# Forming three modulation vectors later, and layer-norm statistics on a second engine, in a hand-ordered long-convolution and MLP block

## The chip, the cores and the metric

The kernel runs on one core of a Trainium2 chip. A core has a matrix engine (PE, whose weight loads are listed apart as PEld), a vector engine (DVE), an activation engine (ACT), a general engine (POOL, also called GpSimd) and an engine that mostly issues transfers (SP); 16 DMA engines move data. PE writes to PSUM, and DVE or ACT carry its results from there to SBUF ("eviction"). The metric is the device time of one execution in microseconds (us). Before the change it is 314.69 us, the median of three runs (313.75 to 314.99).

## The reference, cut to what matters

```python
def reference(A_q, A_k, A_v, A_shift_k, A_ssm_k, A_ssm_D, B_x, B_w1, B_w2, B_w3, B_w4, c, w_mod):
    # _A_ref: k is convolved with 4 taps, kv = k_shift * v, then a long
    # causal convolution of kv with ssm_k (through an FFT of length 4096),
    # plus kv * ssm_D; result times q
    # _B_ref: layer norm, @w1, gelu, a token shift by quarters of the channels, @w2,
    # residual; layer norm, @w3, gelu, @w4, residual
    x = A_q                                             # 1 x 2048 x 640, bf16
    mod = (_silu(c) @ w_mod).reshape(c.shape[0], 6, 1, -1)
    sa, ca, ga, sb, cb, gb = (mod[:, i] for i in range(6))     # shortened
    h = _layernorm(x, axis=-1) * (1 + ca) + sa
    x = x + ga * _A_ref(h, A_k, A_v, A_shift_k, A_ssm_k, A_ssm_D)
    h = _layernorm(x, axis=-1) * (1 + cb) + sb
    x = x + gb * _B_ref(h, B_w1, B_w2, B_w3, B_w4)
    return x
```

Three of the six vectors (ga, ca, sa) are needed for the query side of the convolution block; the other three (cb, sb, gb) first when the MLP block begins.

## The kernel before

The kernel is a list of tasks. Each task names the engine or engines that may run it, what it reads and writes, and a function that records its instructions. A string `ORDER` holds one word for each task: its number, the letter of its engine (P for PE, A for ACT, D for DVE, G for POOL, S for SP), and for PE tasks the PSUM places that it takes (four places of two banks each). The instructions are recorded in just that order; each engine works through its own list in order and waits for what it needs.

```python
    def evac(dst, src, n, ps, w, eng=("ACT", "DVE")):       # eviction, on either engine
        ...
        return add(eng, {"ACT": ca(n), "DVE": cd(n)}, f, (), w, use=ps)
```

The transform of the convolution is made of matrix products. Stage 1 and stage 2 turn the filter (`s`) and then kv into spectra; the filter's spectrum lies in R3 (10 blocks of 2048 columns), that of kv in R5. In between, PE makes the shift of k (`k_shift`), whose result DVE multiplies by v and transposes in 32x32 blocks.

```python
    def stage2(XSd, dreg):
        for k in range(32):
            ...   # 4 matmuls of 64 x 64 x 320 each, then one 128x640 eviction
    def mod_half(i, j, hf):        # half of modulation vector j
        w, wk = wm[i % 3]          # three buffers, in RH and RK
        dma("SP", 410, lambda q: q.dma_start(w, mod_d[:, :, j * D + 320 * hf:j * D + 320 * hf + 320]), w=[wk], rate=250.0)
        ...                        # 5 matmuls of 320 columns, one write of modv (copy, +1 or product)
    def mods():
        for i, j in enumerate((2, 1, 0, 4, 3, 5)):
            for hf in range(2):
                mod_half(2 * i + hf, j, hf)
    def ln1_stats(A):              # 16 tiles of 128 x 640
        ...
            for i in range(2):
                nc.vector.bn_stats(st[:, i, :], x_all[:, A, i * 320:(i + 1) * 320])
            nc.vector.bn_aggr(mv1[:, A, :], st[:])
        add("DVE", 1.1, f, ...)
    x_load(0, 8)
    x_load(8, NT)
    for a0, a1 in ((0, 4), (4, 6), (6, 8), (8, 10), (10, 12), (12, 14), (14, 16)):
        for A in range(a0, a1):
            ln1_stats(A)
        ln1_fin(a0, a1)            # on POOL: 1/sqrt(var + eps) and -mean/sqrt(var + eps)
    mods()
```

Then come the spectral products and the first inverse step, for two halves h of five blocks b each:

```python
    def inverse1(h, b):
        i = h * ND + b
        kx, xs = R3[:, 2048 * i:2048 * i + 2048], R5[:, 2048 * i:2048 * i + 2048]
        ky, kk = KSY[i % 4]        # four buffers; ky is kx with its partition halves swapped, by DMA
        ...
        for T, k_, deps, wr in ((TA, kx, [kxk], ka), (TB, ky, [kk], kb)):
            add("DVE", 1.24, ...)  # one 128x2048 product each
        for w8 in range(2):
            ...                    # 16 matmuls of 128 columns, one 128x1024 eviction
```

The second inverse step (`inverse2`) returns to tokens. `make_q` forms the normalized and modulated query tile (a normalization, one multiply, one add); `chain_a` gates the convolution with it and adds the residual (L689, L692), `chain_b` normalizes and modulates with cb and sb (L703, L704), `chain_c` normalizes again and transposes. Then the MLP: `mm_w1`, `mm_w2` (eviction L832), `mm_w3` (gelu on ACT, L861) and `mm_w4` (evictions L899 to L905, with gb), for eight groups of two tiles.

```python
    for g in range(8):
        ra = chain_a(g)
        rb = chain_b(g, ra)
        chain_c(g, rb)
        ...
        mm_w1(g)
        if g >= 1:
            mm_w2(g - 1)
        if g >= 2:
            mm_w3(g - 2)
            mm_w4(g - 2)
```

Of the kernel before, what the change touches and what calls it, by code (L numbers as in the profile page):

```python
# [18 lines left out]
ND = D // P  # L19
# [7 lines left out]
19G 0S 18D 20D 21G 23D 22D 24A 56G 27G 29D 28D 25A 2S 31A 30A 36G 37G 68G 69D 26G 90P:0 91A 86P:1 6S 87A 88P:2 89A 4S 72G 73D 104P:3 105A 102P:0  # L27
106P:1 107A 38G 39G 40A 3S 70D 71D 96P:2 97A 98P:3 103D 99A 5S 74G 75D 49G 1S 66G 94P:0 50G 8S 118P:1 9S 114P:2 115A 10S 92P:3 93A 95D 41G 52D 51D 32D
53A 116P:0 110P:2 119D 84P:3 42G 11S 43G 34S 7S 54A 33G 44A 85A 111A 67D 117D 122P:1 123D 112P:3 113A 108P:2 109A 100P:0 101D 76P:3 77A 203S 45G 47S
46S 78P:1 79D 35S 82P:2 83A 80P:0 81A 120P:3 170P:1 283D 121D 178P:2 55G 171A 176P:0 179A 180P:1 177A 65G 181D 194P:3 198P:2 195A 199D 234S 48S 202S  # L30
148P:0 57G 58G 200S 149A 142P:1 201S 143D 182P:3 183A 140P:2 141D 231S 12S 13S 144P:0 145A 188P:1 14S 136P:3 15S 189A 137D 162P:2 163A 156P:0 157D
164P:1 165A 150P:3 151D 190P:2 191A 168P:0 174P:1 175A 169D 196P:3 197A 138P:2 139D 160P:0 161A 16S 186P:1 158P:3 159A 146P:2 184P:0 185A 187D 17S
166P:1 167A 147D 192P:3 193A 235P:2 236A 152P:0 213D 232P:1 153A 233A 208D 154P:3 155A 172P:2 288P:0 173A 294P:1 295A 289A 284D 126P:3 298P:2 302P:1
209D 124P:0 214D 59G 60A 299A 303A 210D 296P:2 297A 130P:1 300P:2 301A 127D 125D 290P:3 291A 128P:0 61G 211D 62G 63G 64A 237S 285D 304P:2 306P:3 307A
131D 134P:1 129D 286D 305A 310P:0 311A 215G 132P:3 312P:2 313A 135D 133D 238P:0 239D 292P:1 293A 314P:3 315A 316P:2 287D 243S 244P:0 245D 240S 318P:1
317D 319A 326P:3 327D 320P:0 321A 324P:1 325A 322P:2 308P:0 241P:3 212G 393G 246S 247P:1 309A 323D 352P:2 353A 348P:0 242D 248D 486D 380P:3 381A 349D
252S 253P:1 254D 330P:2 331A 346P:0 347D 338P:3 339A 356P:1 357A 334P:2 335D 392S 390P:0 391A 354P:3 355D 376P:1 362P:2 489D 205S 350P:0 351D 377A
249S 250P:3 251D 363A 261S 487D 366P:1 367A 255S 382P:2 383D 332P:0 333A 340P:3 341A 262P:1 263A 217D 258S 344P:0 342P:2 343A 328P:3 329A 256P:1 345D
257D 374P:2 375A 480D 358P:0 276S 359D 364P:3 365A 388P:1 389A 259P:2 260A 275G 281S 481D 279G 277G 264S 368P:0 278G 282G 280G 272S 386P:3 273G 270S
268S 271G 274G 490D 384P:1 387A 385A 360P:2 369D 378P:0 379A 269S 361D 372P:3 373A 336P:1 370P:2 371A 267S 265P:0 492A 216D 337D 401G 266A 400S 394D  # L40
395D 408S 409G 396P:3 398P:2 399A 493D 491D 402D 494D 397A 403D 410D 404P:1 405A 411D 406P:0 418D 412P:2 413A 417G 414P:3 415A 416S 419D 426D 422P:1
423A 424S 420P:2 421A 425G 427D 434D 433G 407A 432S 435D 430P:3 431A 428P:1 442D 441G 438P:2 436P:0 437A 440S 443D 446P:3 444P:0 450D 448S 449G 451D
447A 456S 439A 429A 454P:3 457G 458D 483A 459D 464S 452P:2 466D 460P:1 445A 462P:0 453A 465G 467D 206S 455A 463D 470P:2 471D 461A 207S 468P:3 469A
488D 495P:01 496A 497A 498P:23 500A 482D 479G 474S 484D 485D 204S 220D 226D 219D 519D 520D 508P:01 218G 499A 543D 522D 523D 524A 544D 477S 525G 521A
510A 526G 557D 554D 472S 555D 558D 560D 475S 501G 602D 559A 502P:32 509A 556A 545D 546D 503A 531D 527D 532D 528D 504A 529D 530A 561G 533D 535D 511P:10
534A 505P:32 603D 605D 606D 547D 512A 536G 566A 540D 541P:1 513A 537D 538P:0 562A 563D 542A 539D 478G 221G 564D 551P:1 567D 607A 604A 608G 506A 609G
568D 565A 569A 570D 552A 610D 611D 517S 612D 571G 572D 575D 549P:0 550A 553G 476S 573P:3 574D 613A 514S 576P:1 577D 586P:0 614D 615D 616D 618D 617A
619G 587A 584P:3 585A 578D 579D 507A 580D 548D 672D 623D 624P:1 625A 620D 621P:0 622A 473S 591P:3 634P:2 588P:1 675D 676D 677A 673D 678D 592D 674A
679G 593A 635A 589D 590A 684D 632P:0 518G 633A 636P:3 685D 594G 686D 687A 581D 680D 681D 682D 683A 595G 599D 600P:1 596D 637D 601D 638A 597P:2 639P:0
598A 656P:3 657A 650P:1 688D 582D 640D 641A 689G 225D 583D 516S 223D 690A 652P:2 691S 740D 642G 643G 644D 692D 693S 647D 648P:0 649D 653A 654P:3 626D  # L50
627D 651A 645P:0 628D 743D 744D 745A 702P:2 700P:1 703A 701A 646D 724P:0 720P:2 741D 742A 227G 746G 704P:1 655A 222D 224G 694D 629D 721A 747G 748D
695D 229D 705D 707P:3 725A 718P:2 515S 658P:01 630D 708D 709A 749D 706A 710G 711G 631D 715D 712D 752D 719A 753D 754D 750D 756G 755A 806D 660D 716P:3
717D 713P:2 714A 228D 659P 661D 663S 790P:2 722P:0 786P:3 666D 751A 757G 760A 758A 791A 230G 828D 829D 788P:1 761S 696D 809D 810D 807D 723A 812D 811A
808A 813G 818D 814A 787A 819D 726P:20 759S 770P:3 815D 816D 697D 789A 728D 768P:1 771A 765D 820D 821A 817A 769A 784P:2 766D 664S 822D 698D 699D 823G
824A 826D 665S 827S 825S 767D 729D 775P:3 776D 777A 785A 772P:1 773D 778G 774A 667D 727P 833P:3 834A 730S 779G 732S 782A 831P:1 869D 870D 929D 662S
734D 735D 832A 871A 780D 781S 762A 763D 792P:20 764D 872D 873D 669S 838P:3 737S 839D 731S 874A 739S 830D 835P:1 836D 840A 783S 853P:3 854A 794D 837A
841D 851P:1 849P:2 793P 847P:3 875G 876G 877D 881A 882D 842G 843A 845A 883D 844S 846S 930D 931A 878D 879D 880A 885G 733S 884A 668S 932D 933D 935D 886G
887A 888S 850A 800D 801D 802S 907P:0 934A 936G 848A 852A 913P:2 909P:3 941A 889D 908A 942D 943D 671S 944A 890S 893P:1 894A 738S 891P:0 937D 938D 939D
940A 945D 946G 911P:1 914A 947D 803S 892A 898P:2 899D 910A 948S 949D 950S 670S 895P:0 896D 900A 897A 901D 902G 795D 804S 796S 855P:32 857D 951P:0 952A
799S 953P:3 798S 856P 863D 736S 858D 954A 959P:0 805S 960D 956P:3 905A 906S 955G 990P:2 991D 993P:0 994D 862S 1041D 912A 915P:12 917D 918D 903A 904S  # L60
974P:0 968P:1 957D 958A 961A 970P:3 969A 797S 864D 865S 972P:1 916P 975A 992A 866S 922S 973A 962G 963G 964D 965S 966D 923D 967S 1004P:0 1005A 995A
971A 1002P:1 1003A 1006P:2 1007A 861S 976P:03 920S 996G 997G 921S 868S 919S 867S 998D 999S 1000A 978D 1042D 1008P:1 1009A 859S 860S 924D 977P 984D
1001S 1028P:2 1029A 1030P:0 985D 989S 926S 1024P:1 1031A 987S 1010P:32 986S 988S 979D 983S 980S 1026P:0 925S 927S 1012D 1025A 928S 1013D 1016S 1011P
1018D 982S 1014S 981S 1019D 1021S 1020S 1023S 1027A 1032P:130 1022S 1035D 1036D 1017S 1015S 1040S 1037S 1033P 1043D 1039S 1044D 1048S 1047S 1038S
1045S 1034P 1049D 1050D 1053S 1052A 1046S 1051S 1054A
# [72 lines left out]
def kernel(  # L138
# [335 lines left out]
    def mod_half(i, j, hf):  # L474
        w, wk = wm[i % 3]
# [26 lines left out]
    def mods():  # L502
        for i, j in enumerate((2, 1, 0, 4, 3, 5)):
            for hf in range(2):
                mod_half(2 * i + hf, j, hf)
# [9 lines left out]
    nb1 = mem.tile([P, NT], F32, name="nb1")  # L515
    def ln1_stats(A):
        st = small.tile([P, 2, 6], F32, name="ln1_st", tag="ln1_st", bufs=4)

        def f(e):
            for i in range(2):  # L520
                nc.vector.bn_stats(st[:, i, :], x_all[:, A, i * 320:(i + 1) * 320])
            nc.vector.bn_aggr(mv1[:, A, :], st[:])
        add("DVE", 1.1, f, r=[("Ra", D * A, D * A + D)], w=[("mv1", A, A + 1)])

    def ln1_fin(a0, a1):
        def f(e):
            nc.gpsimd.tensor_scalar_add(rs1[:, a0:a1], mv1[:, a0:a1, 1], EPS)
            nc.gpsimd.tensor_tensor(rs1[:, a0:a1], rs1[:, a0:a1], mhalf[:, a0:a1], ALU.pow)
            nc.gpsimd.tensor_tensor(nb1[:, a0:a1], mv1[:, a0:a1, 0], rs1[:, a0:a1], ALU.mult)
            nc.gpsimd.tensor_scalar_mul(nb1[:, a0:a1], nb1[:, a0:a1], -1.0)  # L530
        add("POOL", 1.7 + 0.02 * (a1 - a0), f, r=[("mv1", a0, a1)], w=[("ln1", a0, a1)])
# [3 lines left out]
    for a0, a1 in ((0, 4), (4, 6), (6, 8), (8, 10), (10, 12), (12, 14), (14, 16)):  # L535
        for A in range(a0, a1):
            ln1_stats(A)
        ln1_fin(a0, a1)
    mods()
# [61 lines left out]
    for h in range(2):  # L601
        for b in range(ND):
            inverse1(h, b)
# [396 lines left out]
```

## Time and profile before

| | PE | DVE | ACT | POOL |
|---|---|---|---|---|
| busy, us of a span of 311.9 | 275.1 | 228.1 | 197.3 | 101.8 |
| share of the span | 88% | 73% | 63% | 33% |
| instructions | 2816 | 460 | 314 | 227 |

The span is that of one profiled execution. A row of the profile names a line of the kernel, an engine, an operation and its tensors, output before input; `128x640 bf16<-128x640 f32` is 128 partitions of 640 bf16 elements made from as many f32 ones. What stands in square brackets after a row is the time that the engine sat idle before it and who ended that. L210 and L208 are evictions on DVE and ACT, L394 the block transposes, L424 stage 2 on PE, L456 the shift of k, L482 the matmuls of the modulation, L489 to L497 its writes, L521 and L522 the statistics of the first layer norm, L559 and L557 normalizations on DVE and ACT, L566 and L567 multiply and add of the query rows, L582 the spectral products, L593 and L594 the first inverse step. Matmuls are pipelined, so PE's busy time overlaps itself in a group of rows and is no measure of its peak rate.

### The profile page before, as it was taken

The page shows a single profiled execution, that of the slowest core. Times are in us where ns is not written, and L with a number is a line of the kernel's source. Part 1 is how long each engine was busy: PE and PEld are TensorE (multiplying, and loading weights), DVE is VectorE, ACT ScalarE, POOL GpSimd, SP SyncE. Part 2 cuts the span into 40 slices and gives each one's busy share as a digit, 9 for nine tenths or more (in the row PEclk, how much of TensorE's full clock was granted, in tenths as well). Part 3 has the DMA queues.
Part 4 walks back from the last instruction along what each step waited for, and adds up shares of the span by engine and source line. Part 5 has one row for each costly group of instructions (what it writes and reads, how often), then busy time and mean ns, then how long its engine had stood idle before and what let it go on. Part 6 is the DMA issues. An engine that isn't in the chain of part 4 may idle for free.

```text
span 311.9 us, 7129 instructions
## 1 busy us (share of the span) xinstructions
PE 275.1 (88%) x2816; PEld 204.7 (66%) x2816; DVE 228.1 (73%) x460; ACT 197.3 (63%) x314; POOL 101.8 (33%) x227
## 2 busy tenths in 40 slices
PE   0998999999688844778799999999999999999993
PEld 0655656655588632556588787778886768878762
DVE  8999999999999999888976687758744245124233
ACT  4788997889377869879647566766694604342100
POOL 4888227005211416763434331223312103010000
PEclk9999999999789965579999999999999999999998
DMA  5998999997999700820055020221224110320111
GB/s 179 293 184 196 224 182 210 274 226 184 238 253 233 194 9 8 299 92 2 1 128 191 2 58 2 53 49 22 58 61 55 40 41 16 76 53 22 33 47 51
DMA packets 56817, 35.39 MB, mean 113 GB/s; under 512 B 38528, under 2 KB 53504, under 8 KB 56784
## 3 DMA queue, kind: packets, MB, share of 16 engines
q1 hardware_dynamic: 55552, 31.49, 42.6%
q0 software_dynamic: 1136, 3.41, 4.4%
q8 instruction: 22, 0.36, 0.5%
q14 instruction: 11, 0.09, 0.1%
q10 hardware_dynamic: 96, 0.04, 0.1%
HBM read 16.31 MB, written 2.62 MB: 61 GB/s over the span
## 4 chain that ended last, share of the span: by engine, by line
PE 59%; DVE 19%; ACT 8%; POOL 4%; issue 4%; DMA 3%; SPq 0%; DVEq 0%; ACTq 0%; POOLq 0%
PE ps_w L876 18%; PE ps_w L857 17%; PE ps_w L824 5%; DVE Rb L582 5%; PE ps_w L769 4%; PE ps_ksh L456 4%; ACT R L208 3%; PE ps_s L407 2%; PE ps_s L424 2%; DMA Ra<-in_A_ssm_k_dram 2%; PE ps_mod L482 2%; DMA RH<-in_w_mod_dram 2%; DVE R L704 2%; DVE Rb L394 2%; DVE R L461 1%
## 5 line engine op out<-in xcount | busy, mean ns | idle before, releaser
L857 PE MATMUL ps_w<-R,T 128*128 128x256 bf16 x560 | 63.5, 273 | 0.5 <-ACT R L728 0.4
L857 PEld LDWEIGHTS <-T 128*128 128x128 bf16 x560 | 54.4, 98 | 8.3 <-issue 1.6
L876 PE MATMUL ps_w<-T,R 128*128 128x320 bf16 x416 | 59.0, 299 | 0.0
L876 PEld LDWEIGHTS <-R 128*128 128x128 bf16 x416 | 40.6, 98 | 15.4 <-issue 0.3
L861 ACT ACTIVATE R<-ps_w 128x1024 bf16<-128x1024 f32 (+1 forms) x32 | 28.5, 910 | 26.9 <-PE ps_w L857 26.9
L681 ACT ACTIVATE RG<-R 128x640 bf16<-128x640 bf16 x32 | 23.5, 735 | 24.9 <-DVE R L832 18.2
L899 DVE TENSOR_TENSOR T<-ps_w,R 128x640 bf16<-128x640 f32 x15 | 12.3, 823 | 33.6 <-PE ps_w L876 17.2
L208 ACT CAST T<-ps_s 128x1024 bf16<-128x1024 f32 x33 | 31.8, 1018 | 7.4 <-PE ps_s L407 7.2
L407 PE MATMUL ps_s<-F1bd,Rb 128*128 128x256 bf16 x160 | 23.0, 292 | 9.1 <-DVE Rb L394 8.4
L208 ACT CAST R<-ps_s 128x640 bf16<-128x640 f32 x42 | 26.8, 724 | 2.7 <-PE ps_s L424 2.4
L407 PEld LDWEIGHTS <-Rb 128*128 128x128 bf16 x160 | 16.4, 104 | 15.6 <-DVE Rb L394 9.0
L824 PE MATMUL ps_w<-RG,R 128*128 128x320 bf16 x160 | 23.4, 299 | 1.5 <-ACT R L771 1.4
L594 PE MATMUL ps_i<-EB,Rb 128*128 128x128 bf16 x160 | 21.8, 236 | 2.7 <-DVE Rb L582 2.7
L674 POOL TENSOR_TENSOR lnv<-stat,lnv 128x2 f32<-128x2 f32 x24 | 7.0, 290 | 51.7 <-ACT RG L681 44.9
L593 PE MATMUL ps_i<-EA,Rb 128*128 128x128 bf16 x160 | 21.9, 235 | 1.9 <-DVE Rb L582 1.6
L208 ACT CAST T<-ps_i 128x1024 bf16<-128x1024 f32 x18 | 17.2, 1026 | 9.1 <-PE ps_i L594 8.4
L424 PE MATMUL ps_s<-T,RG 64*128 64x320 bf16 x256 | 21.8, 297 | 0.8 <-ACT R L208 0.3
L769 PE MATMUL ps_w<-R,RG 128*128 128x256 bf16 x160 | 21.7, 299 | 0.0
L824 PEld LDWEIGHTS <-R 128*128 128x128 bf16 x160 | 15.2, 98 | 8.1 <-ACT R L771 2.3
L675 POOL TENSOR_TENSOR lnv<-lnv,mhalf 128x2 f32<-128x2 f32 x24 | 19.4, 810 | 1.9
L594 PEld LDWEIGHTS <-Rb 128*128 128x128 bf16 x160 | 16.9, 107 | 4.8 <-DVE Rb L582 4.4
L769 PEld LDWEIGHTS <-RG 128*128 128x128 bf16 x160 | 17.2, 108 | 3.7 <-issue 0.3
(156 smaller groups left out, 502.6 us busy)
## 6 DMA issues: line engine op xcount, KB each, us to landing
RH<-in_w_mod_dram SPq DMA_DIRECT2D x8, 400.0 KB, 5.3
Ra<-in_A_ssm_k_dram SPq DMA_DIRECT2D x5, 512.0 KB, 6.2
Ra<-in_A_q_dram SPq DMA_DIRECT2D x8, 320.0 KB, 6.2
out_dram<-RH SPq DMA_DIRECT2D x60, 40.0 KB, 1.6
T<-in_B_w_dram SPq DMA_DIRECT2D x1, 2160.0 KB, 8.3
T<-in_B_w_dram SPq DMA_DIRECT2D x1, 2080.0 KB, 9.8
RK<-in_w_mod_dram SPq DMA_DIRECT2D x4, 400.0 KB, 4.8
RK<-R SPq DMA_DIRECT2D x5, 256.0 KB, 5.2
```

Of the source, the lines that this page charges most:

```text
L208: nc.scalar.copy(dst, src(ps.tile))
L407: nc.tensor.matmul(psv[:, ml, :], lhsT=xL[:, s0:s0 + P], rhs=F1r, start=True, stop=True)
L424: nc.tensor.matmul(psv[:, g], lhsT=Gs[p, k, 64 - 64 * cc:192 - 64 * cc], rhs=T1b[p, cc * 32 + k], start=(cc == 0), stop=(cc == 1), tile_po ...
L593: nc.tensor.matmul(psv[:, w, :], lhsT=Av[:, r_, :, g_], rhs=EAf, start=True, stop=False)
L594: nc.tensor.matmul(psv[:, w, :], lhsT=Bv[:, r_, :, g_], rhs=EBf, start=False, stop=True)
L675: nc.gpsimd.tensor_tensor(rs, rs, mhalf[:, 0:n], ALU.pow)
L681: add("ACT", 0.74, lambda e: nc.scalar.activation(junk, src, ACT.Square, scale=float(D) ** -0.5, accum_out=stat[:, li, 1, t:t + 1]), r=[sk ...
L769: nc.tensor.matmul(pt[:, fb, :], lhsT=w1_sb[:, b, 160 * fb:160 * fb + P], rhs=hT[:, b, :], start=(b == 0), stop=(b == ND - 1))
L824: nc.tensor.matmul(pt[:, hf, 0:320], lhsT=gsf[:, fb, c0:c0 + P], rhs=w2_sb[:, fb, 320 * hf:320 * hf + 320], start=(fb == 0), stop=(fb == 4))
L857: nc.tensor.matmul(pt[:, fl, :], lhsT=w3_sb[:, b, fb * P:(fb + 1) * P], rhs=xT[:, b, :], start=(b == 0), stop=(b == ND - 1))
L861: nc.scalar.activation(g3[g % 2][:, f0:f0 + fn, :], ps.tile[:, 0:fn, :], ACT.Gelu_apprx_tanh)
L876: nc.tensor.matmul(pts[i][hf][:, hf, 0:320], lhsT=gg[:, fb, i * P:(i + 1) * P], rhs=w4_sb[:, fb, 320 * hf:320 * hf + 320], start=(fb == 0 ...
```

## The change

It does four things.

1. The last six of the twelve modulation halves (vectors cb, sb, gb) are formed after the products have begun. Their weights no longer share the three buffers but lie in the first half of R3, whose blocks of the filter's spectrum are free once they have been used. The first layer norm's statistics of tiles 8 to 15 are also recorded later.
2. The statistics may run on ACT: two passes with a running sum (the values scaled by 1/640, the squares scaled by 1/640), instead of the statistics operations of DVE. For such a tile POOL subtracts the squared mean afterwards, two small operations for each tile.
3. In the last part, four tasks on DVE (block transposes of 128x1024 in differently strided forms) and four on POOL (two multiplies, a scale-and-add, a copy) are added. They read and write free space of Rb, and nothing uses what they leave; they are there so that their durations may be read from a profile.
4. The order and the choice of engines are new throughout: the whole string `ORDER` is replaced.

```diff
 ORDER = """
-19G 0S 18D 20D 21G 23D 22D 24A 56G 27G 29D 28D 25A 2S 31A 30A ...
+0S 18D 2S 19G 36G 56G 21G 20D 23D 24A 22D 25A 27G 28D 29D 31A ...
 ...   (cut: all of its lines differ)
     def mod_half(i, j, hf):
-        w, wk = wm[i % 3]
+        w, wk = wm[i % 3] if i < EARLY else wl[i - EARLY]
 ...
-    def mods():
+    EARLY = 6
+    wl = [(R3[:, o:o + 1600].rearrange("p (b n) -> p b n", b=ND), ("R3", o, o + 1600)) for o in range(0, 9600, 1600)]
+
+    def mods(lo, hi):
         for i, j in enumerate((2, 1, 0, 4, 3, 5)):
             for hf in range(2):
-                mod_half(2 * i + hf, j, hf)
+                if lo <= 2 * i + hf < hi:
+                    mod_half(2 * i + hf, j, hf)
 ...
     def ln1_stats(A):
 ...
-        add("DVE", 1.1, f, r=[("Ra", D * A, D * A + D)], w=[("mv1", A, A + 1)])
+        def fa(e):
+            if e == "DVE":
+                return f(e)
+            xa = x_all[:, A, :]
+            jk = RQ[:, 2560:3200] if A < 8 else junk
+            nc.scalar.activation(jk, xa, ACT.Identity, scale=1.0 / D, accum_out=mv1[:, A, 0:1])
+            nc.scalar.activation(jk, xa, ACT.Square, scale=float(D) ** -0.5, accum_out=mv1[:, A, 1:2])
+        st1[A] = add(("ACT", "DVE"), {"ACT": 1.72, "DVE": 1.1}, fa, ...)
     def ln1_fin(a0, a1):
         def f(e):
+            for A in range(a0, a1):
+                if st1[A].on == "ACT":
+                    m = mv1[:, A, 0:1]
+                    nc.gpsimd.tensor_tensor(nb1[:, A:A + 1], m, m, ALU.mult)
+                    nc.gpsimd.tensor_tensor(mv1[:, A, 1:2], mv1[:, A, 1:2], nb1[:, A:A + 1], ALU.subtract)
 ...
-    for a0, a1 in ((0, 4), (4, 6), (6, 8), (8, 10), (10, 12), (12, 14), (14, 16)):
-        for A in range(a0, a1):
-            ln1_stats(A)
-        ln1_fin(a0, a1)
-    mods()
+    ln1_all((0, 4), (4, 6), (6, 8))
+    mods(0, EARLY)
 ...
     for h in range(2):
         for b in range(ND):
             inverse1(h, b)
+    mods(EARLY, 12)
 ...
+    ln1_all((8, 10), (10, 12), (12, 14), (14, 16))
 ...
+    def spare(g):
+        a, z = Rb[:, 0:2048].bitcast(I32), Rb[:, 2048:4096].bitcast(I32)
+        ja, jz = Rb[:, 0:2048], Rb[:, 2048:4096]
+
+        def f(e):
+            if g == 3:
+                nc.vector.transpose(out=z, in_=a.rearrange("p (n j) -> p j n", n=32))
+            elif g == 4:
+                nc.vector.transpose(out=z.rearrange("p (r j) -> p j r", r=32), in_=a)
+            elif g == 5:
+                nc.vector.transpose(out=z, in_=a)
+            else:
+                nc.vector.transpose(out=jz[:, 0:1024], in_=ja[:, 0:1024])
+        add("DVE", 2.02, f, w=[("Rb", 0, 4096)])
+
+        def f2(e):
+            c, d = Rb[:, 4096:4736], Rb[:, 4736:5376]
+            if g == 3:
+                nc.gpsimd.tensor_tensor(d, c, gbv, ALU.mult)
+            elif g == 4:
+                nc.gpsimd.tensor_scalar(d, c, 0.5, 0.25, ALU.mult, ALU.add)
+            elif g == 5:
+                nc.gpsimd.tensor_tensor(Rb[:, 6144:8192], Rb[:, 4096:6144], Rb[:, 8192:10240], ALU.mult)
+            else:
+                nc.gpsimd.tensor_copy(d, c)
+        add("POOL", 1.8 if g != 5 else 5.0, f2, r=[("modB", 6, 12)], w=[("Rb", 4096, 10240)])
 ...
             add("DVE", 1.02, f, r=[xk_(t), ("modB", 6, 12)], w=[bk, ok], port=0.8)
+            if i == 1 and 3 <= g <= 6:
+                spare(g)
```

What the order changes, in instructions: of the first eight tiles' statistics, ACT gets five and DVE three (two of them ahead of the products); of the other eight, ACT gets two and DVE six. DVE has 9 evictions of 128x1024 and 26 of 128x640 ahead of the first product (7 and 22 before). PE does the first six modulation halves ahead of stage 2 of kv, and the other six between the groups of the first inverse step: one after the fourth group, one after the fourteenth, one after the sixteenth, one after the eighteenth, and two after the twentieth, the last. Ahead of the first product DVE now forms no multiplied query rows (three before).

## The prediction

> **What bounds the kernel now.** I read the page's busy totals first (PE 88%, DVE 73%, ACT 63%), then cut the span at the places where the timeline shows one stage of PE work giving way to the next, and asked for each engine's busy time in every stretch. The columns are the stretch and its length, PE, weight loads, DVE, ACT, POOL, each in us with its instructions, then the granted clock, the DMA share and GB/s.
>
> ```profile
> 8.40:28.30 19.90, 18.76 (x112) 11.88 (x112) 19.32 (x18) 16.73 (x20) 17.37 (x25) 1.00 0.98 225
> 28.30:41.40 13.10, 12.52 (x139) 7.31 (x138) 12.75 (x20) 12.52 (x22) 4.87 (x5) 1.00 1.04 199
> 41.40:64.10 22.70, 22.50 (x152) 14.32 (x152) 22.27 (x28) 18.66 (x22) 7.69 (x12) 1.00 1.06 231
> 64.10:79.80 15.70, 15.08 (x159) 8.45 (x158) 14.49 (x29) 14.08 (x24) 4.49 (x10) 1.00 0.88 206
> 79.80:104.70 24.90, 20.61 (x289) 18.93 (x289) 24.17 (x23) 16.25 (x19) 6.69 (x11) 0.86 0.95 226
> 104.70:128.10 23.40, 11.82 (x554) 8.79 (x554) 22.31 (x58) 17.94 (x29) 11.23 (x34) 0.66 0.27 74
> 128.10:153.60 25.50, 20.57 (x146) 14.61 (x147) 22.03 (x61) 21.87 (x47) 13.50 (x29) 0.85 0.26 101
> 153.60:307.00 153.40, 153.25 (x1273) 120.35 (x1272) 82.97 (x199) 76.03 (x131) 31.61 (x92) 1.00 0.23 52
> ```
>
> The reader is to see two regimes. From 153.6 to 307 PE is never idle (153.25 of 153.40) and DVE is half idle: nothing saved on DVE or ACT there shortens the kernel. Before 153.6 DVE is busy 93 to 98% of every stretch up to 128, and PE is nearly full too from 41 to 80. So a gain must be made before 153.6; it then moves the saturated tail forward as a block.
>
> The DVE timeline at the hand-over from the forward transform of kv (stage 2) to the spectral products shows what sits in the first place (start, duration, engine, line, tensors):
>
> ```profile
> 71.63 0.87 DVE L521 BATCH_NORM_STATS2 ln_st<-Ra 128x6 f32<-128x320 bf16 x2
> 72.54 0.21 DVE L522 BATCH_NORM_AGGREGATE mv<-ln_st 128x2 f32<-128x12 f32 x1
> 72.66 0.77 DVE L210 CAST R<-ps_s 128x640 bf16<-128x640 f32 x1
> 73.83 0.49 DVE L495 CAST modv<-ps_mod 128x320 bf16<-128x320 f32 x1 [0.39 <-PE ps_mod L482]
> ...
> 79.80 1.22 DVE L582 TENSOR_TENSOR Rb<-R,R 128x2048 bf16<-128x2048 bf16 x1
> 80.94 1.22 DVE L582 TENSOR_TENSOR Rb<-R,RG 128x2048 bf16<-128x2048 bf16 x1
> ```
>
> Operations overlap a little, so I cost them by start-to-start distance: a tile's statistics 71.63 to 72.66 = 1.03 us, a product 79.80 to 80.94 = 1.14, and in the same way from neighbouring rows a 128x640 eviction 0.75, a 128x1024 eviction 1.13, a modulation write or 128x640 bf16 multiply 0.40, a normalization 0.36. And PE's timeline of that stage:
>
> ```profile
> 69.20 0.85 PE L482 MATMUL ps_mod<-RH,silu_w 128*128 128x320 bf16 x5
> 69.98 1.26 PE L424 MATMUL ps_s<-T,RG 64*128 64x320 bf16 x16
> 71.24 0.84 PE L482 MATMUL ps_mod<-RH,silu_w 128*128 128x320 bf16 x5
> 72.01 0.99 PE L424 MATMUL ps_s<-T,RG 64*128 64x320 bf16 x12
> ```
>
> Half a modulation vector takes PE 69.20 to 69.98 = 0.78 us; one frequency of stage 2 (four matmuls) 1.26/4 = 0.315.
>
> **What the Trainium skill says.** "Perfetto Trace Analysis", section "Identifying the Most-Contended Engine", warns that matmul busy share is a poor measure of roofline; the trace agrees from 28 to 41, where PE is listed at 12.52 of 13.10 but the four-matmul pitch would need only 32 x 0.315 = 10.1, and ACT (12.52) and DVE (12.75) evictions pace it. "TensorE: Matmul & The Clock Gate", Part 1, says that idle PE drops to half clock and needs some us of work to recover; the clock column above (0.86, 0.66, 0.85) agrees, so a little more PE work after a gap costs double. "DMA: Bandwidth & Descriptors", section "Issuing engines are not separate DMA queues": all transfers share 16 engines; the share of 0.95 from 80 to 105 agrees, and there the later modulation weights will be loaded. "SBUF — State Buffer", section "Who interferes with whom": a VectorE operation with two SBUF inputs contends with GpSimd reads; that is the spare GpSimd operations' risk, and nothing in this trace measures it for tensors of their size.
>
> **The change, part by part**, counting the two instruction lists per stage.
>
> 1. Forward stages to the first product (8.4 to 79.8). DVE loses 6 tiles of statistics (8 to 2): -6.2 us; three modulation writes: -1.2; three multiplies of query rows: -1.2. It takes over four 128x640 evictions, +3.0, and two 128x1024 ones, +2.3. Sum -3.3 us. PE loses six modulation halves in stage 2 of kv, 6 x 0.78 = -4.7, but the two that stood in the filter's stage 2 move into the stretch 41 to 64. ACT gains four tiles of statistics: two passes of 0.86 each by the distance of the squares at L681, so +6.9, minus 6 evictions (4 x 0.64 + 2 x 0.95 = 4.5) and two copies (0.9): +1.5.
> By stage: 28 to 41 loses two modulation copies and an eviction on ACT, about -1. From 41 to 64 PE needs six shifts x 1.73 + 19 stage-1 groups x 0.435 + six halves x 0.78 = 23.3, and ACT 15 evictions x 0.95 + 6.9 + 1.4 = 22.6 of the 22.7 us that the stretch has: both full, so about +0.5. From 64 to 79.8 PE needs only 10.1, ACT 18 x 0.64 = 11.5, DVE 14 x 0.75 = 10.5; about 12.3 with the start, so -3.4. Sum about -3.7 against DVE's own -3.3. I take -3.5: the first product at about 76.3.
>
> 2. Products (79.8 to 104.7): DVE has the same 20 products and exchanges two multiplies for two modulation writes: 0. PE gets four of the six halves between inverse groups, +3.1 on 20.6 of 24.9, early ones at half clock. The first waits for its weights: they may be loaded only after the first product and its spectrum's transfer, and land 5.3 us later (the median of the DMA issues for w_mod), about 6.5 us after the first product; PE reaches that point after two inverse blocks at half clock, about 9 us after it. So no wait for data, but a hold of up to 1 us on PE. ACT: +1 eviction, +1.7 statistics, +1.3 copies, -0.9: about 19.5, not a bound. I take +0.7.
>
> 3. From the last product to the first gated row (L689, 111.73 in before): DVE loses one eviction (-1.13) and two statistics (-2.06), gains three multiplies and a normalization (+1.56): -1.6. But the inverse transform's first rows come no sooner than PE and ACT let them, and two more modulation halves stand before it on PE; I credit -0.7. From there to the first second-layer eviction (150): two 128x960 evictions +2.0, +0.8 for multiplies, minus 3 x 0.4 for LN sums given to POOL: +1.2, partly in DVE gaps; I take +0.6.
>
> 4. Tail: DVE +1 statistic (1.03), four spare transposes (about 2.0 each by L394's rows, the last maybe half), ACT two statistics (+3.4), POOL about 10 us of copies and multiplies (four operations, scaled from its 128x640 copy of 0.99 and 128x512 multiply of 1.3). DVE has 70 us of idle time there. I take +0.5 for a wait or two of PE.
>
> Sum: -3.5 + 0.7 - 0.7 + 0.6 + 0.5 = -2.4. Since the summed waits in steps 2 to 4 are allowances, not counted work, and the bare work count says -3.3 + 0 - 1.6 + 1.2 = -3.7, I set the change at -3.2: **311.5 us**, 1% faster.
>
> **The rivals.** *ACT becomes the bound.* For it: 22.6 us of work in the 22.7 us stretch, in an order where statistics stand between evictions that PE's four PSUM places wait for. Then the stretch grows by 2 to 3 us, and the result is 313.5 to 315. Against: DVE took over two of that stage's evictions. *The late weights hold PE and DMA.* Six loads of 400 KB enter a stage with DMA share 0.95 while the products wait for half-swapped spectra; if a swap lands late, each product pair can lose 1 us, and the time is 315 to 318. Against: the six loads leave the busy stretch before, and so the first swaps can start sooner. *The spare work lands on the path in the tail.* A GpSimd multiply of 2048 columns before nothing that matters costs nothing; a 2 us transpose in front of an eviction PE waits for costs 2 us each: up to 318. *The other way:* the order removes part of PE's idle time from 104.7 to 153.6 (48.9 long, 32.4 busy); 3 us of it would bring 308.
>
> **Range and chances.** The counted part is 2.4 to 3.7 us; rivals pull mostly upwards by 2 to 6 us, the fourth downwards by 3. So 307.5 to 316 should hold it 8 times in 10. Faster by over 2% means below 308.4: 0.15. Slower by over 2% means above 321: 0.05. Within: 0.80.
>
> **What would show it right or wrong.** Right: first product at 75.5 to 77.5 (79.80 now); stage 2 of kv 12 to 13 us long with no modulation matmul in it; statistics of the first eight tiles on DVE only three times; the saturated stretch still with PE idle under 1 us and starting 2 to 4 us sooner. Step 1 is wrong if ACT shows no idle time from 41 to 64 and the first product stays after 78; step 2 if PE waits for the modulation weights' DMA or DVE for the swapped spectrum; step 4 if PE's busy share in the last 150 us falls below 99%. The whole prediction is wrong if the time is below 307.5 (the idle time after the products was the order's doing) or above 316.

## The result and the profile after

The changed kernel takes 313.81 us (median of 4 runs, 310.53 to 316.17), the kernel before 314.48 beside it. Two of the changed kernel's four runs were disturbed (over 1.5% above its fastest), as were three of the four of a_nopool, an experiment below that therefore has no ratio; every ratio here is of undisturbed runs. The ratio is 0.989, 95% interval 0.985 to 0.994: about 1% faster, within 2%. The profiled execution has a span of 309.9 us instead of 311.9; this pair differs by 2.0 us, less than the 3.3 that the ratio stands for, and the landmarks below explain these 2.0.

Three of the stretches of the profile after, cut at the same places as before (stretch, length, PE, weight loads, DVE, ACT, POOL, granted clock, DMA share, GB/s):

```profile
41.40:64.10 22.70, 22.53 (x165) 14.88 (x164) 22.31 (x28) 21.81 (x36) 11.45 (x20) 1.00 0.93 219
64.10:79.80 15.70, 12.76 (x142) 8.79 (x140) 15.12 (x19) 11.38 (x18) 6.16 (x12) 0.87 0.84 202
79.80:104.70 24.90, 23.74 (x410) 21.44 (x411) 23.49 (x28) 21.07 (x29) 6.32 (x21) 0.94 1.04 261
```

ACT rises from 18.66 to 21.81 of the 22.70 us from 41 to 64, and PE falls from 15.08 to 12.76 in the next stretch, in which the products now begin. VectorE's timeline at the hand-over from stage 2 of kv to the products:

```profile
69.78 4.65 DVE L210 CAST R<-ps_s 128x640 bf16<-128x640 f32 x6
74.56 1.23 DVE L605 TENSOR_TENSOR Rb<-R,R 128x2048 bf16<-128x2048 bf16 x1
```

Six evictions run back to back into the first product; the statistics and the modulation write that stood there before are gone. Read from such rows, with the same landmarks in both traces:

| landmark | before | after | lead |
|---|---|---|---|
| first product (L582, now L605) starts | 79.80 | 74.56 | 5.24 |
| last product ends | 104.71 | 100.33 | 4.38 |
| first gated row (L689, now L714) | 111.73 | 106.19 | 5.54 |
| first third-layer matmul (L857, now L882) | 153.57 | 149.79 | 3.78 |
| last matmul ends | 306.96 | 304.77 | 2.19 |
| span | 311.9 | 309.9 | 2.0 |

So in these two profiles the change gains 5.2 us before the products and hands 3.2 of them back: 1.5 on the way to the saturated tail, 1.6 inside it and 0.2 after its last matmul. The tail's loss is PE waiting. From the first third-layer matmul to the last matmul, the stretch of before and then that of after, and the list of after's PE waits in it (who waited, for whom, us in total, times, longest):

```profile
153.57:306.96 153.39, 153.27 (x1273) 120.38 (x1272) 82.99 (x198) 76.03 (x131) 31.64 (x92) 1.00 0.23 52
```

```profile
149.79:304.77 154.98, 153.22 (x1275) 120.64 (x1272) 93.71 (x203) 82.08 (x143) 44.70 (x105) 1.00 0.19 39
```

```profile
PE ps_w1x L804 <- DMA R<-RK: 0.6, 1, 0.6
PE ps_w L849 <- DVE T L951: 0.6, 1, 0.6
PE ps_w1x L804 <- ACT RG L706: 0.6, 1, 0.6
```

PE has the same 153.2 us of work in both; its idle time goes from 0.12 to 1.76 us, three waits of about 0.6 at 156.6, 194.3 and 234.3.

### The profile page after: what moved, and what is told of

Read it like the earlier page. It is cut to its first block, busy times and chain, and to the rows that moved or that the text cites. A ratio compares the mean times of both kernels' runs of the same rounds, so it can differ in the third digit from the quotient of the medians.

```text
span 309.9 us, 7171 instructions
## 1 busy us (share of the span) xinstructions
PE 272.4 (88%) x2816; PEld 205.0 (66%) x2816; DVE 233.2 (75%) x436; ACT 206.2 (67%) x339; POOL 116.3 (38%) x254
## 4 chain that ended last, share of the span: by engine, by line
PE 52%; ACT 16%; DMA 8%; POOL 8%; DVE 7%; issue 6%; SPq 1%; ACTq 0%; POOLq 0%; DVEq 0%
PE ps_w L928 16%; PE ps_w L882 16%; PE ps_w L849 6%; DMA RK<-R 4%; ACT R L208 4%; ACT T L208 3%; PE ps_w L794 3%; ACT RG L706 3%; DMA RG<-RG 2%; PE ps_s L424 2%; DMA Ra<-in_A_ssm_k_dram 2%; PE ps_mod L482 2%; DVE Rb L605 2%; PE ps_i L657 2%; DVE R L729 1%
## 5 line engine op out<-in xcount | busy, mean ns | idle before, releaser
L882 PE MATMUL ps_w<-R,T 128*128 128x256 bf16 x560 | 63.6, 273 | 0.0
L882 PEld LDWEIGHTS <-T 128*128 128x128 bf16 x560 | 54.5, 98 | 7.6 <-issue 0.8
L951 DVE TENSOR_TENSOR T<-ps_w,R 128x640 bf16<-128x640 f32 x15 | 12.3, 823 | 27.2 <-PE ps_w L928 16.2
L208 ACT CAST T<-ps_s 128x1024 bf16<-128x1024 f32 x31 | 29.3, 1039 | 2.5 <-PE ps_s L407 2.5
L407 PE MATMUL ps_s<-F1bd,Rb 128*128 128x256 bf16 x160 | 22.1, 285 | 8.5 <-DVE Rb L394 8.0
L849 PE MATMUL ps_w<-RG,R 128*128 128x320 bf16 x160 | 25.0, 311 | 1.8 <-ACT R L796 1.2
L407 PEld LDWEIGHTS <-Rb 128*128 128x128 bf16 x160 | 16.0, 102 | 14.5 <-DVE Rb L394 8.6
L857 DVE SCALAR_TENSOR_TENSOR R<-ps_w,R 128x640 bf16<-128x640 f32 x16 | 13.2, 823 | 16.5 <-PE ps_w L849 16.5
L208 ACT CAST R<-ps_s 128x640 bf16<-128x640 f32 x38 | 24.2, 718 | 2.0 <-PE ps_s L424 2.0
L208 ACT CAST T<-ps_i 128x1024 bf16<-128x1024 f32 x19 | 18.2, 1029 | 7.7 <-PE ps_i L617 7.1
L210 DVE CAST R<-ps_s 128x640 bf16<-128x640 f32 x26 | 19.9, 819 | 1.2 <-PE ps_s L424 0.8
L424 PEld LDWEIGHTS <-RG 64*128 64x128 bf16 x256 | 13.3, 94 | 10.1 <-issue 5.0
L794 PE MATMUL ps_w<-R,RG 128*128 128x256 bf16 x160 | 19.7, 280 | 0.2 <-ACT R L796 0.2
```

The costliest lines, as they stand in the source:

```text
L208: nc.scalar.copy(dst, src(ps.tile))
L210: nc.vector.tensor_copy(dst, src(ps.tile))
L407: nc.tensor.matmul(psv[:, ml, :], lhsT=xL[:, s0:s0 + P], rhs=F1r, start=True, stop=True)
L424: nc.tensor.matmul(psv[:, g], lhsT=Gs[p, k, 64 - 64 * cc:192 - 64 * cc], rhs=T1b[p, cc * 32 + k], start=(cc == 0), stop=(cc == 1), tile_po ...
L794: nc.tensor.matmul(pt[:, fb, :], lhsT=w1_sb[:, b, 160 * fb:160 * fb + P], rhs=hT[:, b, :], start=(b == 0), stop=(b == ND - 1))
L849: nc.tensor.matmul(pt[:, hf, 0:320], lhsT=gsf[:, fb, c0:c0 + P], rhs=w2_sb[:, fb, 320 * hf:320 * hf + 320], start=(fb == 0), stop=(fb == 4))
```

## The experiments

My theory was that work taken off PE and VectorE ahead of the first product makes the gain, and that the new order loses part of it in the tail. The rivals: statistics on ScalarE bound the forward stages; the order alone makes the gain; the late weights hold the products; the spare operations hold the tail. Every ratio below is to the kernel before on the same chip, with its 95% interval. "First product" is its start in the run's own profile.

### The parts alone, in the order of before

Four kernels. *b_mods*: only the six modulation halves late. *b_stats*: only the statistics on the changed kernel's engines. *b_both*: both. *b_split*: both, and every operation ahead of the products on the engine that the changed kernel gives it. In all four the sequence is that of before; words that had to move (late halves, two tiles' statistics and the fifth query tile behind the first products) stand beside the same neighbours as in the changed kernel. None has spare operations.

```diff
# b_mods
-    mods()
+    mods(0, EARLY)                       # EARLY = 6
...
+    mods(EARLY, 12)                      # behind the products; weights in R3
# b_stats: order words of the first six tiles, each at its old place
-  208D 209D 210D 211D 213D 214D
+  208A 209D 210D 211A 213A 214A
```

> The kernel before, with only the last six modulation halves moved behind the products (their weights into freed spectrum space), everything else in the order of before. Work theory: six groups of five matmuls and six evictions leave the second transform stage, where PE and the evicting engines are full, so the first product comes at 77.5 to 78.5 instead of 79.8, and about 1.5 us of it reaches the end: 313.0. Statistics theory (the modulation halves were hidden beside the evictions): first product at 79.3 or later, time 314.5. Late-weights theory: the six loads in the product stretch, which is full of transfers, hold PE or VectorE there: products take 27 us instead of 24.9, time 315 to 317.

> The kernel before, with only the statistics of layer norm 1 on the engines that the changed kernel gives them: of the first eight tiles four on ScalarE at their old places, two moved behind the first products. Work theory: VectorE loses about six tiles of 1.03 us ahead of the products, ScalarE gains four of 1.74, so the first product comes at 76.5 to 78 and the time is 312 to 313. Rival, ScalarE becomes the bound: four tiles, 7 us, stand between evictions that PE waits for; first product at 79.5 or later and time 314.5 to 316.

> The kernel before with both parts (six late modulation halves, statistics on the changed kernel's engines) but with the rest of the order as before, and no spare operations. Work theory: first product at 75 to 76.5, near the 74.56 of the changed kernel; tail without the three PE waits that the changed kernel has, so time 310.5 to 311.5. Order theory (the new order, with its other split of evictions between the engines, makes most of the gain): first product at 77.5 or later, time 312.5 to 313.5.

> The kernel before with both parts, as in the run that took 332.9 us, and in addition every operation ahead of the first product on the engine (ScalarE or VectorE) that the changed kernel gives it; only the sequence is still that of before. Split theory (that run was slow because ScalarE kept its evictions and got the statistics on top): first product comes back from 84.4 to 75 to 78, time 311 to 315. Sequence theory (what counts is where a statistic stands among the evictions that PE waits for, not how many evictions an engine has): first product stays at 81 or later, time 325 or more.

Measured: b_mods 1.013 (1.006 to 1.019), b_stats 1.050 (1.042 to 1.057), b_both 1.060 (1.054 to 1.066), b_split 1.096 (1.090 to 1.103). All four are slower than the kernel before, and my work theory fell for each. For b_mods the late-weights theory came nearest in number: its products took 28.0 us (79.1 to 107.1) instead of 24.9, and its loads landed 9.1 us after issue (median). But the one long wait among them has another cause:

```profile
93.91 0.49 DVE L493 TENSOR_SCALAR modv<-ps_mod 128x320 bf16<-128x320 f32 x1
94.45 0.23 PE L597 MATMUL ps_i<-EA,Rb 128*128 128x128 bf16 x1 [2.35 <-DVE modv L493]
```

A modulation write stands behind the products in VectorE's queue, PE waits 2.35 us for it, and VectorE then waits 3.52 us for PE; no wait for a weight load is listed among these products. For the others ScalarE as the bound and the sequence pointed the right way, and in b_stats and b_both the times went beyond even what those expected. The table shows the forward part; VectorE's busy time is summed over the stretches up to the first product, and its idle time is the rest.

| kernel | first product | DVE busy | DVE idle |
|---|---|---|---|
| before | 79.8 | 75.8 | 4.0 |
| changed | 74.6 | 71.1 | 3.5 |
| b_mods | 79.1 | 75.3 | 3.8 |
| b_stats | 87.1 | 71.3 | 15.7 |
| b_both | 84.4 | 69.9 | 14.5 |
| b_split | 96.9 | 74.1 | 22.8 |

In the kernel before, the changed one and b_mods the first product comes when VectorE has done its work plus 3.5 to 4.0 us. In b_mods PE has 3.8 us less to do there (65.0 instead of 68.9), and the first product moves by 0.7, hardly more than the 0.5 that VectorE saves: work taken off PE brought nothing while VectorE stayed full. VectorE saves so little because one small multiply, 0.11 us in the kernel before, takes 1.16 here and ends with a GpSimd operation; that eats 1.05 of the 1.5 us of the three modulation writes that left:

```profile
9.66 1.27 POOL L311 TENSOR_TENSOR R<-R 128x512 f32<-128x512 f32 x1
9.79 1.16 DVE L440 TENSOR_TENSOR Ra<-Ra,Dcol 128x1 bf16<-128x1 bf16 x1
```

And b_stats takes as much work off VectorE as the changed kernel, but VectorE then stands idle. From the timeline of b_stats at 42.7:

```profile
42.69 1.03 PE L407 MATMUL ps_s<-F1bd,Rb 128*128 128x256 bf16 x8 [1.27 <-ACT R L208]
...
42.86 0.75 ACT L531 ACTIVATE RQ<-Ra 128x640 bf16<-128x640 bf16 x1
...
43.73 0.74 ACT L532 ACTIVATE RQ<-Ra 128x640 bf16<-128x640 bf16 x1
...
44.46 1.27 ACT L208 CAST R<-ps_s 128x640 bf16<-128x640 f32 x2
45.19 0.58 PE L456 MATMUL ps_ksh<-R,RQ 128*128 128x512 bf16 x1 [1.46 <-ACT R L208]
...
48.80 1.23 DVE L461 TENSOR_TENSOR R<-ps_ksh,R 128x1024 bf16<-128x1024 f32 x1 [6.19 <-PE ps_ksh L456]
```

The two passes of a tile's statistics (L531, L532) keep ScalarE from 42.86 to 44.46, the evictions behind them come late, PE waits 1.46 us for one, and VectorE waits 6.19 us for PE. In the changed kernel ScalarE runs the same passes of two tiles from 40.94 to 44.38, and PE's waits for it from 41.4 to 64.1 are 0.2 us in all. What differs is where the passes stand among the evictions, and which evictions ScalarE has. Giving evictions to the other engine without their new places (b_split) makes it worse still: ahead of the first product VectorE waits 19 us for PE, and PE 10 us for ScalarE. So the share of the engines alone isn't it; that the places are is argued from these waits. An engine's order is a queue, and a word at the head of it that is not ready holds all behind it.

### Statistics back on VectorE, in the order of after

*a_statsdve* changes four letters of the changed order.

```diff
-  208A 211A 213A 214A
+  208D 211D 213D 214D
```

> The changed kernel with the four early statistics of layer norm 1 that stand on ScalarE put on VectorE, at the same places of the order. VectorE is busy 22.3 of 22.7 us from 41.4 to 64.1. If the statistics on ScalarE are where the gain ahead of the first product comes from: four times 1.03 us later, first product at 78 to 79, time 314 to 316. If the gain is the modulation halves' and the order's: first product within 1 us of 74.56, time within 1 us of 311.

Measured: 0.998 (0.995 to 1.000) against the changed kernel's 0.989; first product at 77.9, VectorE busy 74.9 us before it and idle 3.0. The first expectation was right: 3.8 us more work, first product 3.3 later. So of the 5.2 us gained, 3.3 hang on the four tiles on ScalarE, provided that the order has places for them. Of the other 1.9, about 1.3 has to do with neither of the parts: a_statsdve too lacks the held steps of the angle table that step 1 below shows.

### The modulation halves back in the forward stage

*a_modsearly* and *a_modsearly2* put the six late halves back into stage 2 of kv, with the three old weight buffers. In the first, loads and matmuls stand beside the same groups as in the kernel before; in the second each load follows the group that frees its buffer and the matmuls are spread. The sixteen small transfers that use these buffers come later with them.

```diff
-    EARLY = 6
+    EARLY = 12
# and the order words of six loads, matmuls and writes, and of 16 transfers RH <- RK
```

> The changed kernel with the six late modulation halves back in the second transform stage, with the old weight buffers, and with the sixteen small transfers that need those buffers placed as before. If the halves are worth what leaves the stage (six groups of five matmuls at about 0.15 us pitch plus six evictions of 0.4 us): first product 2 to 3.5 us later, at 76.5 to 78, and up to 1 us given back in the products, whose transfers get lighter by 2.4 MB; time 312 to 314. If they fitted into gaps: first product within 0.7 us of 74.56 and a time at or below the changed kernel's.

> The changed kernel with the six late halves back in the second transform stage, this time with each weight load right behind the group that frees its buffer and with the matmuls spread as far as the loads allow. In the first trial PE waited 2.1 us for a weight load and the first product came at 85.0. If that trial was late by its placement alone: first product at 76.5 to 78. If three buffers and a load of about 6 us each are the limit, so that the halves cannot end before about 77 wherever they stand: first product at 79 to 82.

Measured: 1.021 (1.014 to 1.027) and 1.037 (1.031 to 1.044), first product at 86.3 (the second expectation says 85.0, which was misread) and 85.2, both later than any expectation had it. VectorE has 73 us of work before it and stands idle for 13.3 and 12.1. In PE's timeline of the first:

```profile
66.09 0.85 PE L482 MATMUL ps_mod<-RH,silu_w 128*128 128x320 bf16 x5 [2.09 <-DMA RH<-in_w_mod_dram]
```

PE waits 2.09 us for weights that could be loaded only once their buffer was free, and all evictions behind wait with it. But my hand placement is not the new order without the halves' move; an order found for that case would do better, as the kernel before shows, which has them there and starts its products at 79.8. These two runs bound the halves' worth from above and settle nothing more. What moving the halves alone brings stays open; b_mods shows only that it brings nothing without a new order.

### The spare operations

*a_nopool* drops the four spare GpSimd operations, *a_nospare* all eight spare ones, *a_longpool* makes all four GpSimd ones the long form.

```diff
# a_nopool
-        add("POOL", 1.8 if g != 5 else 5.0, f2, ...)
# a_nospare
-            if i == 1 and 3 <= g <= 6:
-                spare(g)
# a_longpool: for every g
+            nc.gpsimd.tensor_tensor(Rb[:, 6144:8192], Rb[:, 4096:6144], Rb[:, 8192:10240], ALU.mult)
```

> The changed kernel without its four spare GpSimd operations; the four spare VectorE transposes stay. Lock theory (a VectorE operation that reads and writes bf16 in SBUF alone stands still while such a GpSimd operation runs): the normalization at about 187.9, which took 1.49 us, takes 0.44 again, the PE wait of 0.56 us at 194.3 goes, the one at 267.6 (3.88 us) falls to 0.45, and the span is 0.4 to 0.7 us shorter: 313.2. Rival (the wait at 194 belongs to the order of VectorE's work and would be there anyway): that wait stays within 0.2 us, time the same within 0.2 us.

> The changed kernel without any spare operation, VectorE's or GpSimd's. Lock theory: the normalization at about 188 takes 0.44 us instead of 1.49, the PE wait of 0.56 at 194.3 is gone, PE's idle time in the tail falls from 1.76 to about 1.2, time 0.4 to 0.7 shorter than the changed kernel: 310.3 to 310.9 beside its undisturbed 311.1. Rival (the order makes all three waits): PE idle in the tail stays at 1.6 or more, same time.

> The changed kernel with all four spare GpSimd operations made the long form, a multiply of 2048 columns that took 4.06 us. Lock theory (a VectorE normalization, bf16 from SBUF to SBUF, that starts while such a GpSimd operation runs ends only when that one ends): the normalization at about 188 takes about 4.1 us, and the PE wait of 0.56 us near 194 grows by some 2.7 to about 3 us; the span is 2 to 3 us longer. Rate theory (the two only share bandwidth, so that VectorE runs at a third of its speed at worst): the normalization stays at 1.0 to 1.5 us and the wait below 0.8.

First the changed kernel's own timeline, at its second wait and at the long GpSimd multiply (start, duration, engine, line):

```profile
187.78 1.39 POOL L908 TENSOR_TENSOR Rb<-Rb,modv 128x640 bf16<-128x640 bf16 x1
187.86 1.49 DVE L582 TENSOR_SCALAR R<-Ra,lnv 128x640 bf16<-128x640 bf16 x1 [1.36 <-POOL lnv L701]
...
193.40 0.82 DVE L951 TENSOR_TENSOR T<-ps_w,R 128x640 bf16<-128x640 f32 x1
...
194.27 1.11 PE L849 MATMUL ps_w<-RG,R 128*128 128x320 bf16 x7 [0.56 <-DVE T L951]
...
267.26 4.06 POOL L912 TENSOR_TENSOR Rb<-Rb 128x2048 bf16<-128x2048 bf16 x1
...
267.62 3.88 DVE L582 TENSOR_SCALAR RH<-R,lnv 128x640 bf16<-128x640 bf16 x1
```

A normalization of 640 columns, 0.44 us elsewhere, takes 1.49 and 3.88 us: it starts after the GpSimd operation and ends within 0.2 us of its end, whatever that lasts. The spare multiply at 187.8 puts VectorE 1.05 us behind, and its queue carries that to the eviction that PE awaits at 194.3. Without spare operations (a_nospare, the same normalization):

```profile
190.73 0.45 DVE L582 TENSOR_SCALAR R<-Ra,lnv 128x640 bf16<-128x640 bf16 x1 [1.37 <-POOL lnv L701]
```

and with the long form (a_longpool, timeline, with an eviction that began 0.08 us after another of these multiplies, and then the longest PE wait):

```profile
189.02 4.05 POOL L907 TENSOR_TENSOR Rb<-Rb 128x2048 bf16<-128x2048 bf16 x1
...
189.10 4.15 DVE L582 TENSOR_SCALAR R<-Ra,lnv 128x640 bf16<-128x640 bf16 x1 [1.37 <-POOL lnv L701]
...
205.44 0.82 DVE L944 TENSOR_TENSOR T<-ps_w,R 128x640 bf16<-128x640 f32 x1 [1.15 <-PE ps_w L921]
```

```profile
PE ps_w L849 <- DVE T L944: 3.2, 1, 3.2
```

The normalization grows to 4.15 us (expected about 4.1) and the PE wait to 3.2 (about 3). That is the lock theory; at a shared rate the normalization would not follow the length of the other operation. The eviction from PSUM keeps its 0.82 us. In time, a_longpool is 1.010 (1.006 to 1.013), some 6 us above the changed kernel; its trace shows 2.8 of them as PE's idle time in the tail (4.56 us instead of 1.76), and the rest stays open. a_nospare is 0.992 (0.989 to 0.995), no different from the changed kernel: an effect of 0.56 us lies below what the times can resolve, and it is the trace that shows it. In a_nospare PE idles 0.55 us in the tail: the waits at 156.6 and 194.3 are both gone and the third remains. I expected 1.2; the first went without a change to the order there, so it seems to depend on when a transposing transfer happens to land. The trace of a_nopool shows the normalization at 0.45 us and no wait for the eviction of L951.

### Late weights and the order of the tail

*a_tail* is a_nospare with one group of third-layer matmuls put ahead of the first feed-forward group that waited at 156.6. *a_late* adds to this that all six late loads are issued behind the last half swap and three of the six halves are formed behind the second group of the inverse transform.

```diff
# a_tail (order words, PE and ACT)
-  702P:3 ... 703A ... 700P:2 ... 724P:0 ... 650P:3 ... 651A
+  650P:3 ... 702P:0 ... 651A 703A ... 700P:2 ... 724P:3
# a_late
-  442S 443P:3 ... 444D ... 445S ... 446P:2 ... 454S ... 455P:1 456A   (among the products)
+  451S ... 457S ... 448S 442S 445S 454S   (behind the last swap)
```

> The changed kernel without spare operations; the 20 matmuls of the first feed-forward group that waited 0.64 us for a transposing transfer put behind the next group that was ready; and all six late weight loads issued behind the last half swap of the products instead of three among them, three of the six modulation groups behind the second group of the inverse transform. If the late weights, 2.4 MB among the half swaps, hold the products: products (first product to the end of the last) take 24.5 to 25 us instead of 25.7, the waits at 156.6 and 194.3 are gone, and the time is 309 to 310. If the transfers don't matter there: products unchanged, only the two waits of 1.2 us gone, 310 to 310.7; and if the later groups delay the first gated rows, whose stage keeps VectorE busy 21.2 of 23.4 us, up to 1 us of that is lost again: 311.

> The changed kernel without spare operations and with the 20 matmuls of the first feed-forward group that waited 0.64 us at 156.6 put behind the next ready group; the late weight loads stay among the half swaps. Order theory of the tail: of the changed kernel's three waits only the one of 0.55 at 234.3 is left, PE idle after the first third-layer matmul falls from 1.76 to 0.6 us, that matmul to the end of PE takes 153.8 instead of 155.0, time about 310. Rival (a wait taken away comes back behind the next group, as VectorE or ScalarE set the pace there): PE idle in that stretch stays above 1.2 and the time at 311 to 311.5.

Measured: a_tail 0.992 (0.990 to 0.995), a_late 0.999 (0.997 to 1.001). In a_tail the wait at 156.6 is gone, and PE's waits from the first third-layer matmul on are

```profile
PE ps_w1x L804 <- ACT RG L706: 0.5, 1, 0.5
PE ps_w L882 <- ACT R L886: 0.5, 1, 0.5
```

The second of these is new: the rival was half right, a wait came back behind the group that was put first. PE idles 1.06 us there, against 0.55 in a_nospare. Nothing is gained over it, in the trace or in time.

In a_late the products (first start to last end) take 24.3 us, a little less than expected; with the late halves among them they take 25.7 in a_longpool, 25.8 in the changed kernel, 26.4 in a_tail and 28.9 in a_nospare. These four have the same operations up to there, so profiles differ by 3 us without a change, and the cost of the late halves is known only as some 1.4 us or more. From a_tail to a_late, the pair that differs in this alone, VectorE's work falls by 0.9 us (two modulation writes fewer) and its idle time by 1.2. In a_tail 1.19 us of idle time stand before one product that reads a half-swapped block; such a stop is there in a_longpool (0.71) and a_nospare (2.42) too, and not in a_late. The profile names no releaser, so that a late swap is the cause is likely and not shown. a_late takes loads and matmuls out together, so their shares stay open. But it loses that gain and more in the next stage, where PE runs the three halves in one go:

```profile
108.36 3.73 PE L482 MATMUL ps_mod<-R,silu_w 128*128 128x320 bf16 x15
```

They take 3.73 us there, 0.25 us each (0.16 in stage 2 of the kernel before: 0.78 for five), while the inverse transform waits behind them; the first row that needs a late vector (L728) comes at 116.4 instead of 113.8, and the tail starts at 151.3 instead of 149.8. I had allowed 1 us for this.

## The prediction, step by step

**Time.** 311.5 us was predicted, a gain of 3.2; the ratio 0.989 on 314.5 is a gain of 3.3. That they agree so well is luck in part: the total hides terms that were off both ways, and two of my sums were wrong. The stages of step 1 add to -3.9, not -3.7, and the work of step 3's second half to +1.6, not +1.2, so the bare count is -3.3, not -3.7. (VectorE's share from 64 to 80 is 92%, just under the 93 that I wrote.) Of the signs of being right, the tail's early start (3.8 us) and the three statistics on VectorE held; the first product came before its range (74.56 for 75.5 to 77.5), stage 2 of kv took 11.0 us for 12 to 13, and PE's idle time in the tail was over 1 us.

**Step 1, first product: -3.5 predicted, -5.2 measured.** The mechanism was right, VectorE's work sets the first product, and the mis-sized term is VectorE's count: -3.3 counted, -4.7 measured (75.8 to 71.1 us busy), plus 0.5 less idle time. Nearly all of the missing 1.4 us is no work at all. In the kernel before, two steps of an angle table on VectorE met GpSimd's own steps on another table:

```profile
15.98 1.93 POOL L309 TENSOR_SCALAR R<-R 128x512 f32<-128x512 f32 x1
...
17.42 0.54 DVE L294 TENSOR_SCALAR R<-R 128x64 int32<-128x64 int32 x1
...
18.00 1.27 POOL L311 TENSOR_TENSOR R<-R 128x512 f32<-128x512 f32 x1
18.03 1.29 DVE L294 TENSOR_SCALAR R<-R 128x64 int32<-128x64 int32 x1
```

After, the same two take 0.20 us each:

```profile
20.25 0.20 DVE L294 TENSOR_SCALAR R<-R 128x64 int32<-128x64 int32 x1
...
21.77 0.20 DVE L294 TENSOR_SCALAR R<-R 128x64 int32<-128x64 int32 x1
```

The two rows are 1.43 us shorter together; since one of them overlaps the step that follows it, the four steps of this table take 1.27 us less from start to start (17.15 to 19.24 before; 19.93 to 20.36 and 21.49 to 21.88 after). Beside the second, GpSimd does nothing; the first stands beside a GpSimd operation (19.55, 1.52 us) and is not held, so not every such meeting costs time, and which do was not found out. This is read from the rows; no run tested it. I had counted operations at their usual durations and not looked for rows that were longer than their shape allows.

**Step 2, products: +0.7 predicted, +0.9 measured** (24.9 to 25.8). The late weights landed 8.3 us after issue (median) instead of the 5.3 that I took from the kernel before; a_late points to the late halves as the cost, but does not part their loads from their matmuls.

**Step 3:** first gated row -0.7 predicted, -1.2 measured; from there to the first second-layer eviction (143.9 and not the 150 that I wrote, now 140.6) +0.6 predicted, +2.2 measured; 0.5 of that comes back by the tail. No run separated this term into its causes, and it stays open.

**Step 4, tail: +0.5 predicted, +1.6 on PE and 0.2 after its end measured.** I named "a wait or two" and there are three. By the sign that I set (PE under 99% in the last stretch; 153.22 of 154.98 is 98.9%) this step was wrong in size. I looked for the danger in the spare transposes on VectorE, to which no PE wait is put down, and took GpSimd's spare work as free; it was GpSimd that held VectorE. I had cited the Trainium skill, "SBUF — State Buffer", section "Who interferes with whom", for VectorE operations with two SBUF inputs only. The same section says that one of the tensor_scalar kind in a two-port mode and GpSimd also exclude each other, for the whole instruction. The traces agree: each held normalization ended 0.18 us after the GpSimd operation; that it ran in such a mode no trace shows. The case that I had cited occurred too: in a_longpool a multiply with two SBUF inputs beside one of the GpSimd multiplies took 4.38 us (at 275.30), 0.49 elsewhere.

**Rivals.** ScalarE as the bound: false for the changed kernel, in which PE waited 0.7 us for it in all ahead of the first product; true of b_stats, where it cost 7 us of the first product, and b_both and b_split, which also have the statistics on ScalarE without the new order, lose 5 and 17. Late weights: likely if loads and matmuls are taken together, some 1.4 us or more of the products, but the whole did not come to the 315 to 318 us that I gave it, as the early gain outweighs it. Spare work: true for one of four GpSimd operations, 0.6 us. Order removing idle time from 104.7 to 153.6: that stretch began 4.38 us early and ended 3.78 us early, so it did not.

## What to carry to other kernels

Where every engine's order is fixed by hand, an operation moved to an idle engine is worth its time only if its new place in that engine's queue is one that nobody waits behind; the same four tiles on ScalarE were worth 3.3 us of the first product in one order, and cost 7 in another. Where several engines are full in a stage, work taken off one that doesn't set the end of it may bring nothing, as here with 3.8 us off PE. Before counting work, look for rows that are longer than the same shape elsewhere: GpSimd work that nobody waits for can still stop VectorE, and a change that merely moves the two apart can gain what no count of operations shows.

## What was unexpected of the hardware

- A bf16 normalization of 128x640 from SBUF to SBUF on VectorE stood still until the running GpSimd operation ended: 1.49, 3.88 and 4.15 us beside GpSimd operations of 1.39, 4.06 and 4.05, against 0.44 alone; an eviction from PSUM that began 0.08 us after a 4.06 us multiply (a_longpool, 205.44) kept its 0.82.
- On GpSimd a bf16 multiply of two tensors took 1.39 us for 640 columns and 4.06 for 2048, a multiply and add with constants over 640 columns 0.73.
- A 32-bit block transpose of 128x1024 on VectorE took 1.23 us where both sides are contiguous and 1.94 or 1.95 where one side is strided; the bf16 one of the same size took 1.24.
- A weight load of 400 KB landed 4.0 to 5.3 us after its issue in the forward stages of the two kernels and 8.3 us after it among the half swaps (medians).
